# The order of three scales, the first solve's last add and the first T products in a recurrence, expert and feed-forward kernel

## The chip, the cores and the metric

One core of a Trainium2 chip. The metric is device time of the whole program in microseconds, the median of several runs. Three runs of the kernel before gave 1320.99 us as median, with 1320.44 and 1326.19 at the ends.

## The reference

Three stages follow one another: a recurrence over 768 steps for 32 independent heads (4 batches of 8 heads, head size 40), then a mixture of experts with two experts per token, then a feed-forward layer.

```python
for t in range(S):
    y[:, :, t] = einsum('bhd,bhde->bhe', rt, state)
    Sa = einsum('bhde,bhe->bhd', state, at)
    state = state * wt[:, :, None, :] - einsum('bhd,bhe->bhde', Sa, bt)
    state = state + einsum('bhd,bhe->bhde', vt, kt)
...
logits = x @ w_gate + log1p(exp(x @ w_noise)) * noise
top2 = argpartition(-logits, 2)[:, :2]        # two experts per token, relu(x @ w1[e]) @ w2[e]
...
h = x @ w_in
out = (h * tanh(log1p(exp(h)))) @ w_out
```

All of it is computed in float32 precision.

## The kernel before

**The recurrence.** The 768 steps are cut into 24 chunks of 32 steps, and the heads into two groups of 16, so the recurrence proper (`chain`, line 588) is a loop of 48 steps g, two for each chunk. Inside a chunk the 32 steps are coupled by a triangular system; its inverse T turns the chunk into matmuls. Each chunk i goes through these stages, which lie off the loop and have to be ready ahead of it:

- `scale(i)` (line 210) computes running products of the decays w on VectorE with two scans (lines 217 and 221) and a reciprocal (line 220), and multiplies a by them (abd, line 226) and k and b by their inverses (kb, line 230; on VectorE for chunks under 8). Between the last two it issues `load_w` (line 197: two DMAs on SP) for a later chunk into the tile wa that this scale has just read for the last time; for chunks 5, 6 and 7 that is the load for chunks 7, 8 and 9. ScalarE copies the end products into WE (lines 232 and 233), and `decays(i)` (line 237) copies E into Ec (line 240). Scale and decays together are `decayed(i)`.
- `turned(i)` (line 323) is `prods(i)` (line 257: 32 small matmuls on TensorE, line 270, evicted by ScalarE, line 277, one part being sent to DRAM as lscr, line 278), a mask on GpSimd, `turns(i)` (line 288: four groups of four transposes on TensorE, line 294, evicted by ScalarE, lines 300 and 311, one part being sent to DRAM, line 302), the load of a later kb (line 195), and `scale_a(i)` on GpSimd (line 254), which also loads a later AT (line 247).
- `solve_group(k)` (line 390) solves the triangular systems of four chunks at a time on VectorE. It ends with six pairs of a multiplication (line 428) and an add (a reduction along the free axis, line 431). Behind the last add, T is written to DRAM (tscr, line 465), and `tbd(i)` (line 356, the DMAs of line 360) loads it again as diagonal blocks Tbd, four DMAs for each chunk.
- `apply(i)` (line 363) multiplies Tbd with AM on TensorE, in two halves of eight matmuls each (line 377: "T's products"), and ScalarE evicts them into Z (line 379). Step g of the loop starts from Z: `u_mm` (lines 530 and 533), then `s_mm` (line 543), whose result VectorE multiplies by WE into the next state ST (line 548).

**What sets the order.** On TensorE, ScalarE, VectorE and GpSimd the order of the instructions is the order in which the program emits them (`manual_schedule`). On SP, which issues the DMAs, the framework's scheduler orders them by its own estimate of when each is ready. The emission is ruled by a list of positions. Three generators, prepare (scales and products), solve and apply, each give the position of their next piece; `pump(tau)` (line 677) always runs the piece with the lowest position, up to tau. Everything with a position up to t0 = -0.35 is emitted ahead of the loop over g, the rest in slots between the loop's parts.

Ahead of the loop, a piece's position is -1 + x / 42 (`early`, line 314). In the first solve, x is the running sum of the costs that `at` is given in `solve_group`: seven pieces with 0.38 + 0.0083 t t (3.822 in all), eight with 0.6, then 1.2 for each multiplication and each add. So the last two adds stand at x = 20.622 and 21.822, positions -0.5090 and -0.4804. T's products of chunk 0 stand at x = `z0`. The pieces of prepare are listed in `plan`: (1, i, p) is `decayed(i)` and (0, i, p) is `turned(i)` at position p. 

```python
def early(self, x):
    return -1 + x / 42
...
for first, i, at in OPT["plan"]:
    yield at
    for _ in (self.decayed if first else self.turned)(i):
        yield at
...
yield self.tau(at + sg * OPT["zd"]) if i else self.early(OPT['z0'])
```

Behind the recurrence come the experts (`Experts`, with matmuls at lines 1235 and 1254) and the feed-forward layer (`Ffn`, lines 1548 and 1610); the change does not touch them.

Of the kernel before, what the change touches and what calls it, by code (L numbers as in the profile page):

```python
# [24 lines left out]
PR = 8  # L25
NC = S // C
NG = NP * NC
OPT = dict(yd=(), yv=33, gix=(1, 3, 4), ye=(2, 2),  lag2=1, plan=((0, 4, -0.881), (1, 5, -0.499), (1, 6, -0.498), (0, 5, -0.495), (1, 7, -0.493), (0, 6, -0.316), (0, 7, -0.249), (1, 8, -0.020)), dl=0, dk=0, ns=(0, 0), nw=(1, 1), va=1, rb=0, ra=1, kb=0, ry=(2, 2), p1=(0, 0, 0, 1, 1, 1), lw=((4, 2, 2), (6, 6, 6)), fl=((0, 1, 2, 2, 2, 2, 2, 2), (0,) * 8), lag=6, ll=.06, hurry=40, pool=(1, 4), rvpool=False, f=(3, 3, 1, 1, 1, 0), s=(.05, .72), s_1=(-.12, .62), tl=1.9, zl=.96, zd=.32, t0=-.35, nd=3, z0=22)
NW = 2 * PR * (C + 1)
NTB = 2  # L30
GJ = 4
# [34 lines left out]
class Rec:  # L66
# [190 lines left out]
    def prods(self, i):  # L257
# [18 lines left out]
        for out, k in ((ls, 1), (am[:, :, 64:96], 0))[:1 if i < GJ else 2]:  # L276
            nc.scalar.mul(out=out, in_=pv[:, :, k], mul=-1.0)
        (nc.scalar if i < OPT['dl'] else nc.sync).dma_start(out=self.lscr[i // GJ][i % GJ * PR:i % GJ * PR + PR].rearrange("u q t i -> (q t) u i"), in_=ls)

# [8 lines left out]
    def turns(self, i):  # L288
# [12 lines left out]
        self.KN[i] = self.pkn.tile([128, HH * D], F32, name="knd")  # L301
        (nc.scalar if i < OPT['dk'] else nc.sync).dma_start(out=self.KN[i], in_=kn.rearrange("p h d -> p (h d)"))
        if i % 2 == 0:
# [28 lines left out]
    def prepare(self):  # L332
        n = len(self.seq)
        for first, i, at in OPT["plan"]:
            yield at
# [27 lines left out]
    def apply(self):  # L363

        nc = self.nc
        for i in range(len(self.seq)):
            at = 2 * i - OPT["zl"]
            if i and i % GJ == 0:
                yield self.tau(2 * i - OPT["tl"])
                self.tbd(i)  # L370
            self.wants[2] = lambda: 2 if self.solved <= i // GJ else self.ready <= i
            z = self.Z[(i + 2) % 3]
            for sg in range(2):
                yield self.tau(at + sg * OPT["zd"]) if i else self.early(OPT['z0'])
                pt = self.pp.tile([128, 512], F32, name="pp")
# [1332 lines left out]
```

## Time and profile before

| | |
|---|---|
| median of three runs | 1320.99 us (1320.44 to 1326.19) |
| the profiled execution | 1327.01 us, of which the span is 1325.2 us |
| TensorE busy | 1154.2 us (87%) |
| VectorE busy | 872.9 us (66%) |
| ScalarE busy | 704.7 us (53%) |
| GpSimd busy | 573.7 us (43%) |
| granted clock of TensorE, mean | 0.937 of full speed |

The profile is of one execution; its times are microseconds from the start of the span, and the shares of busy time are means over stages with different limits. The recurrence comes first in the span, and its preparation at the very start. Engines in the rows: PE is TensorE, DVE VectorE, ACT ScalarE, POOL GpSimd, SPq the DMA issues of SyncE. "out<-in" are the program's names without buffer numbers; "pp" and "cs" are PSUM tiles. A granted clock of 1.00 is 2.4 GHz, 0.50 is 1.2 GHz.

### The profile page before, as it was taken

How to read it: one execution, taken by the hardware profiler on the slowest of the kernel's cores; microseconds unless marked ns; L12 is line 12 of the kernel's file. 1: busy time of each engine (PE TensorE's matmuls, PEld its weight loads, DVE VectorE, ACT ScalarE, POOL GpSimd, SP SyncE). 2: the span in 40 equal slices, each digit the busy share in tenths (PEclk: the TensorE clock that was granted, in tenths of full speed). 3: DMA queues.
4: the chain of work that ended last, by engine and by line, in shares of the span. 5: the costliest groups of instructions: out<-in, count | busy, mean ns of one | idle time of the engine just before them, and what ended most of it. 6: DMA issues, size and time to landing. Idle time of an engine off the chain costs nothing. (4 is left out here: it accounts for less than half of the span.)

```text
span 1325.2 us, 34053 instructions
## 1 busy us (share of the span) xinstructions
PE 1154.2 (87%) x13902; PEld 1108.1 (84%) x13902; DVE 872.9 (66%) x1601; ACT 704.7 (53%) x1475; POOL 573.7 (43%) x525
## 2 busy tenths in 40 slices
PE   5156788889779797898999999898989999999998
PEld 5146677878678686898999999898989999999998
DVE  8938869595957352646787787585466555665543
ACT  5435566667447365343344344342366766666664
POOL 5223736363336334432244444342355545554331
PEclk9578798999879798899999999898999999999999
DMA  8565585858445657662563564653271111110000
GB/s 237 140 158 130 135 199 136 213 125 205 106 113 107 79 121 125 126 200 76 161 194 113 171 190 131 203 162 123 80 207 31 41 40 31 31 32 19 11 11 21
DMA packets 144989, 156.83 MB, mean 118 GB/s; under 512 B 70954, under 2 KB 113962, under 8 KB 144810
## 3 DMA queue, kind: packets, MB, share of 16 engines
q1 hardware_dynamic: 127594, 120.52, 36.1%
q0 software_dynamic: 10752, 22.32, 6.4%
q10 hardware_dynamic: 6464, 11.54, 3.1%
q8 instruction: 120, 1.97, 0.7%
q14 instruction: 59, 0.48, 0.1%
HBM read 111.20 MB, written 43.12 MB: 116 GB/s over the span
## 5 line engine op out<-in xcount | busy, mean ns | idle before, releaser
L1580 POOL TENSOR_TENSOR gl<-fh,gh 128x1024 fp32r<-128x1024 f32 x46 | 131.0, 2876 | 105.4 <-ACT gh L1596 102.0
L1235 PE MATMUL ph<-xh,w1h 128*128 128x256 f32 (+1 forms) x576 | 160.4, 291 | 8.9 <-issue 8.9
L1235 PE MATMUL ph<-xl,w1h 128*128 128x256 f32 (+1 forms) x576 | 160.1, 291 | 0.0
L1548 PE MATMUL fps<-fxh,ih 128*128 128x256 f32 x576 | 156.4, 286 | 2.0 <-DVE fh L1550 2.0
L1548 PE MATMUL fps<-fxl,ih 128*128 128x256 f32 x576 | 153.8, 281 | 0.5 <-DVE fxl L1091 0.3
L1579 DVE TENSOR_TENSOR fh<-fh,fp 128x1024 f32<-128x1024 f32 x48 | 95.0, 2014 | 60.5 <-ACT fp L1578 60.5
L1254 PE MATMUL py<-w2h,hh 128*128 128x320 f32 x400 | 130.5, 326 | 4.1 <-ACT hh L1087 3.3
L1089 DVE SCALAR_TENSOR_TENSOR hl<-ph,hh 128x512 fp32r<-128x512 f32 (+1 forms) x104 | 69.2, 666 | 89.0 <-ACT hh L1087 88.7
L1254 PE MATMUL py<-w2h,hl 128*128 128x320 f32 x400 | 126.5, 316 | 1.1 <-DVE hl L1089 1.1
L1254 PE MATMUL py<-w2l,hh 128*128 128x320 f32 x400 | 126.3, 316 | 1.3 <-DVE w2l L1091 1.3
L1235 PEld LDWEIGHTS ph<-xh,w1h 128*128 128x128 f32 x576 | 111.8, 194 | 10.0 <-issue 9.8
L1550 DVE COPY fh<-fps 128x512 f32<-128x512 f32 x96 | 64.8, 690 | 79.4 <-ACT fp L1549 74.0
L1610 PE MATMUL fpy<-oh,gl 128*128 128x320 f32 x384 | 114.6, 310 | 0.0
L1610 PE MATMUL fpy<-oh,gh 128*128 128x320 f32 x384 | 114.3, 309 | 0.0
L1610 PE MATMUL fpy<-ol,gh 128*128 128x320 f32 x384 | 113.9, 308 | 0.0
L1235 PEld LDWEIGHTS ph<-xl,w1h 128*128 128x128 f32 x576 | 111.9, 194 | 0.4 <-DVE xl L1091 0.4
L1235 PE MATMUL ph<-xh,w1l 128*128 128x256 f32 (+1 forms) x384 | 111.5, 290 | 0.4 <-DVE w1l L1091 0.4
L1548 PEld LDWEIGHTS fps<-fxh,ih 128*128 128x128 f32 x576 | 109.0, 189 | 2.3 <-DVE fh L1550 2.2
L1548 PEld LDWEIGHTS fps<-fxl,ih 128*128 128x128 f32 x576 | 109.0, 189 | 1.1 <-DVE fxl L1091 1.1
L1548 PE MATMUL fps<-fxh,il 128*128 128x256 f32 x384 | 107.8, 281 | 0.0
L1087 ACT ACTIVATE hh<-ph 128x512 fp32r<-128x512 f32 (+1 forms) x104 | 59.7, 579 | 87.3 <-PE ph L1235 86.2
L1549 ACT ACTIVATE fp<-fps 128x512 f32<-128x512 f32 x96 | 56.0, 596 | 79.3 <-PE fps L1548 75.0
(278 smaller groups left out, 3267.7 us busy)
## 6 DMA issues: line engine op xcount, KB each, us to landing
share<-in_w_dram SPq DMA_DIRECT2D x9, 1280.0 KB
share<-in_w_dram SPq DMA_DIRECT2D x9, 1024.0 KB
wa<-in_wa_dram SPq DMA_DIRECT2D x40, 195.2 KB
knd<-kn SPq DMA_DIRECT2D x24, 320.0 KB
kb<-in_kb_dram SPq DMA_DIRECT2D x40, 192.0 KB
KB<-knd SPq DMA_DIRECT2D x24, 320.0 KB
yb<-y SPq DMA_DIRECT2D x22, 320.0 KB
ST<-in_vn_dram SPq DMA_DIRECT2D x48, 128.0 KB
```

The source lines that it names most:

```text
L1087: nc.scalar.activation(out=hi, in_=src, func=AF.Relu if relu else AF.Copy)
L1089: nc.vector.scalar_tensor_tensor(out=lo, in0=src, scalar=0.0, in1=hi.bitcast(F32), op0=ALU.max, op1=ALU.subtract)
L1235: nc.tensor.matmul(ph[:, m % c], lhsT=a, rhs=b, start=(q == 0), stop=(q == len(ops) - 1))
L1254: nc.tensor.matmul(py, lhsT=a[:, m, ts], rhs=b[:, m], start=(m == 0 and q == 0), stop=(m == FC - 1 and q == 2))
L1548: nc.tensor.matmul(ph[:, i], lhsT=a, rhs=b, start=(q == 0), stop=(q == len(ops) - 1))
L1549: nc.scalar.activation(out=p[:, 2 * m2:2 * m2 + 2], in_=ph, func=AF.Sigmoid, scale=-1.0)
L1550: nc.vector.tensor_copy(h[:, 2 * m2:2 * m2 + 2], ph)
L1579: mul = lambda s: nc.vector.tensor_tensor(out=h[:, s], in0=h[:, s], in1=p[:, s], op=ALU.mult)
L1580: low = lambda s: (nc.vector if last and s.start % 8 else nc.gpsimd).tensor_tensor(out=gl[:, s], in0=h[:, s], in1=gh[:, s].bitcast(F32), o ...
L1610: nc.tensor.matmul(py, lhsT=a[:, m, ts], rhs=w[:, m], start=(q == 0), stop=(q == len(ops) - 1))
```

## The change

Only the table of positions (line 28) is changed; shown are the two entries that differ.

```diff
-plan=((0, 4, -0.881), (1, 5, -0.499), (1, 6, -0.498), (0, 5, -0.495), (1, 7, -0.493), (0, 6, -0.316), (0, 7, -0.249), (1, 8, -0.020))
+plan=((0, 4, -0.881), (1, 5, -0.4512), (1, 6, -0.45), (0, 5, -0.4488), (1, 7, -0.4452), (0, 6, -0.3162), (0, 7, -0.2487), (1, 8, -0.02))
...
-z0=22
+z0=23.2
```

`z0` = 22 is the position -0.4762, and 23.2 is -0.4476. The order of emission between the last two adds of the first solve and the start of the loop is, by these positions:

- before: add (-0.5090), scale 5, scale 6, products and flips of chunk 5, scale 7, last add (-0.4804) with tscr and Tbd of chunk 0, T's products of chunk 0, Tbd of chunk 1;
- after: add (-0.5090), last add (-0.4804) with tscr and Tbd of chunk 0, scale 5, scale 6, products and flips of chunk 5, T's products of chunk 0, Tbd of chunk 1, scale 7.

The pieces at -0.3162, -0.2487 and -0.02 stay in the slots of the loop in which they were.

## Rows read from the trace of the kernel before

**Rows 1.** The page: the span, and VectorE's busy tenths in 40 equal slices (33.1 us each).

```profile
span 1325.2 us, 34053 instructions
...
DVE  8938869595957352646787787585466555665543
```

**Rows 2.** Windows: start:end, length, each engine's busy us and instructions, TensorE's granted clock, DMA share, GB/s.

```profile
59.00:75.00 16.00, 5.17 (x80) 4.15 (x80) 15.79 (x17) 5.42 (x15) 3.62 (x3) 0.50 0.51 129
75.00:81.70 6.70, 0.00 (x0) 0.00 (x0) 0.01 (x1) 0.00 (x0) 0.00 (x0) 0.50 0.63 163
81.70:86.10 4.40, 3.97 (x18) 3.56 (x18) 0.00 (x0) 1.16 (x2) 0.00 (x0) 0.50 0.33 90
86.10:105.00 18.90, 16.88 (x443) 14.53 (x445) 3.45 (x10) 12.77 (x34) 4.88 (x6) 1.00 0.63 159
```

**Rows 3.** Waits, 55 to 100 us: us in total, times, longest.

```profile
PE pp L377 <- DMA Tbd<-tscr: 12.9, 1, 12.9
```

**Rows 4.** Timeline of VectorE: start us, us, line, operation, out<-in [idle before <-releaser].

```profile
59.05 1.24 DVE L217 TENSOR_TENSOR_SCAN E<-wa,d 104x528 f32<-104x528 f32 x1
...
62.38 1.22 DVE L230 TENSOR_TENSOR kb<-kb,R 104x1024 f32<-104x1024 f32 x1
...
68.53 1.25 DVE L217 TENSOR_TENSOR_SCAN E<-wa,d 104x528 f32<-104x528 f32 x1
...
72.67 1.21 DVE L230 TENSOR_TENSOR kb<-kb,R 104x1024 f32<-104x1024 f32 x1
73.80 1.21 DVE L431 TENSOR_REDUCE Tt<-tm 128x128 f32<-128x1024 f32 x1
88.69 0.99 DVE L548 TENSOR_TENSOR ST<-cs,WE 40x320 f32<-40x320 f32 x2 [13.69 <-PE cs L543]
```

**Rows 5.** Timeline of SP's DMA issues, 55 to 130 us.

```profile
62.49 5.67 SPq L195 DMA_DIRECT2D wa<-in_wa_dram  x4
...
72.81 1.00 SPq L195 DMA_DIRECT2D wa<-in_wa_dram  x2
75.04 0.34 SPq L465 DMA_DIRECT2D tscr<-Tt  x1
...
78.41 3.79 SPq L360 DMA_DIRECT2D Tbd<-tscr  x8
```

**Rows 6.** Timeline of TensorE: chunk 5's products and flips, two chunks' T products.

```profile
63.70 1.93 PE L270 MATMUL pp<-kb,abd 40*32 40x64 f32 x64 [18.71 <-issue]
...
67.25 1.63 PE L294 MATMUL pp<-ident,Ec 104*64 104x104 f32 x8
...
81.77 3.70 PE L377 MATMUL pp<-Tbd,share 128*96 128x128 f32 x16 [12.90 <-DMA Tbd<-tscr]
...
99.05 1.11 PE L377 MATMUL pp<-Tbd,share 128*96 128x128 f32 x8
...
100.44 1.04 PE L377 MATMUL pp<-Tbd,share 128*96 128x128 f32 x8
```

**Rows 7.** Timeline of ScalarE, 60 to 89 us: scale 7's copies, T's second eviction, U.

```profile
69.81 0.22 ACT L232 COPY WE<-E 40x16 f32<-40x16 f32 x1 [0.48 <-DVE E L217]
70.04 0.22 ACT L233 COPY WE<-E 40x16 f32<-40x16 f32 x1
70.28 0.62 ACT L240 COPY Ec<-E 104x512 f32<-104x512 f32 x1
...
85.51 0.58 ACT L379 COPY Zt<-pp 96x512 f32<-96x512 f32 x1 [1.13 <-PE pp L377]
86.94 0.86 ACT L533 COPY ST<-cs 32x320 f32<-32x320 f32 x2 [0.85 <-PE cs L530]
```

**Rows 8.** Windows of 1 us: DMA share, the last but one number.

```profile
65.00:66.00 1.00, 1.00 (x27) 0.83 (x20) 0.96 (x2) 0.98 (x4) 0.00 (x0) 0.50 0.15 46
```

**Rows 9.** Windows of the recurrence's first stage, columns as in the second group.

```profile
105.00:210.00 105.00, 79.78 (x1716) 71.63 (x1712) 88.66 (x124) 60.18 (x167) 51.42 (x30) 0.87 0.63 153
...
140.00:160.00 20.00, 12.42 (x246) 11.27 (x241) 17.35 (x18) 7.38 (x21) 14.75 (x7) 0.74 0.44 119
```

More of the change, by code (lines that the diff above doesn't have):

```diff
@@ L27 @@
 NG = NP * NC
-OPT = dict(yd=(), yv=33, gix=(1, 3, 4), ye=(2, 2),  lag2=1, plan=((0, 4, -0.881), (1, 5, -0.499), (1, 6, -0.498), (0, 5, -0.495), (1, 7, -0.493), (0, 6, -0.316), (0, 7, -0.249), (1, 8, -0.020)), dl=0, dk=0, ns=(0, 0), nw=(1, 1), va=1, rb=0, ra=1, kb=0, ry=(2, 2), p1=(0, 0, 0, 1, 1, 1), lw=((4, 2, 2), (6, 6, 6)), fl=((0, 1, 2, 2, 2, 2, 2, 2), (0,) * 8), lag=6, ll=.06, hurry=40, pool=(1, 4), rvpool=False, f=(3, 3, 1, 1, 1, 0), s=(.05, .72), s_1=(-.12, .62), tl=1.9, zl=.96, zd=.32, t0=-.35, nd=3, z0=22)
+OPT = dict(yd=(), yv=33, gix=(1, 3, 4), ye=(2, 2),  lag2=1, plan=((0, 4, -0.881), (1, 5, -0.4512), (1, 6, -0.45), (0, 5, -0.4488), (1, 7, -0.4452), (0, 6, -0.3162), (0, 7, -0.2487), (1, 8, -0.02)), dl=0, dk=0, ns=(0, 0), nw=(1, 1), va=1, rb=0, ra=1, kb=0, ry=(2, 2), p1=(0, 0, 0, 1, 1, 1), lw=((4, 2, 2), (6, 6, 6)), fl=((0, 1, 2, 2, 2, 2, 2, 2), (0,) * 8), lag=6, ll=.06, hurry=40, pool=(1, 4), rvpool=False, f=(3, 3, 1, 1, 1, 0), s=(.05, .72), s_1=(-.12, .62), tl=1.9, zl=.96, zd=.32, t0=-.35, nd=3, z0=23.2)
 NW = 2 * PR * (C + 1)
```

## The prediction

> **What bounds the kernel now.** The page comes first: 1325.2 us of span, and VectorE's slices nearly full from 0 to 80 us, with a hole in the slice after them [rows 1]. The chain that ended last runs through the experts and the feed-forward stage and says nothing of the start, so the start is read from windows. From 59 to 75 us VectorE is busy 15.79 of 16.00 us; from 75.0 to 81.7 us VectorE, TensorE, ScalarE and GpSimd together are busy 0.01 us; then TensorE alone works until 86.1 us [rows 2]. The waits name that hole: TensorE waits 12.9 us at line 377 for the DMA that loads Tbd from tscr [rows 3]. It cannot start without it: the last add of the first solve completes T, T goes to DRAM and comes back as blocks, and no step of the recurrence can run before chunk 0's T products.
>
> The timeline of VectorE shows where that add stands. From 59.05 to 73.88 the engine does the scales of chunks 5, 6 and 7 (five instructions each, the first at 59.05, the last at 72.67 for 1.21 us); the last add runs at 73.80 for 1.21 us; the next VectorE instruction comes 13.69 us later, at 88.69 [rows 4]. So 14.75 us of scales (73.80 - 59.05) lie in front of the one add for which all wait, and 13.7 idle us behind it.
>
> **What the change does, term by term.** Worked out from the numbers of the list, the order on VectorE becomes last add, scales 5, 6, 7. On TensorE it stays: chunk 5's products and flips, then T's products; it is these that have been held together by moving both numbers. On ScalarE the copies of scale 7 move from in front of T's evictions to behind them. On SP the tscr write and the Tbd loads, behind the issues for chunks 7, 8 and 9 until now, come ahead of them in program order.
>
> - **The last add** starts at 59.05 in place of 73.80: 14.75 us earlier, ready at 60.26. By the way through DRAM alone, T's products could start 81.77 - 75.01 = 6.76 us after it [rows 4, 6], at 67.0. The pieces are a tscr issue at 75.04, a first Tbd issue at 78.41 (3.37 later), and T's products 3.36 after that [rows 5, 6].
> - **The scales** come 1.2 us later (one add). That is cheap in itself, but chunk 5's products wait for scale 5 and stand ahead of T's on TensorE. Scale 5's last multiplication ends at 63.60 and the products start at 63.70; the flips end at 67.25 + 1.63 = 68.88 [rows 4, 6]. All of that 1.2 later: TensorE reaches T's products at 70.1. This is later than 67.0, so it decides: **81.77 - 70.1 = 11.7 us earlier**, 3.1 us of the 14.75 given back to chunk 5's products. What hid these products (VectorE's own work on scales 6 and 7) is gone, and this is their price.
> - **ScalarE.** Scale 7's three copies (two for WE, one for Ec) take from 69.81 to 70.90, 1.09 us [rows 7]; now they stand between T's second eviction (end 86.09) and the copy of U into ST (86.94), where 0.85 us are free: **0.24 us lost**. Their input, scale 7's first scan, would be done at 68.53 + 1.25 + 1.2 = 71.0, long before 86.09 - 11.7 = 74.4, so they don't wait.
> - **VectorE behind it.** Scale 7 ends at 72.67 + 1.21 + 1.2 = 75.1, and the first state update is wanted at 88.69 - 11.4 = 77.3: 2.2 us to spare, cost nothing. If that cover is gone, each us of delay of scale 7 beyond 2.2 is paid in full.
> - **SP and the transfers.** Chunk 7's wa loads wait for scale 5's abd product and were issued from 62.49 [rows 5]. They had 6.04 us until scale 7's scan at 68.53, though the transfer share was down to 0.15 between 65 and 66 us [rows 8], so they land about 3 us after the first issue. Now they can go at 63.7 at the earliest, just when the first Tbd load can (78.41 - 14.75 = 63.7). If four Tbd loads go first (eight take 3.79, so 1.9 us [rows 5]), wa goes at 65.6 and lands at 68.6, or by the 6.04 at 71.6, against a scan wanted at 69.7: between 0 and 1.9 us late, within the 2.2 to spare. If wa goes first, Tbd is late by its two issues, 1 us, against 3.1 to spare. Either is taken as 0; the sequence of SP is not written by hand, and is a rival below. Chunk 5's own issues (lscr, knd, the next kb and AT) go 1.2 us later with its products; they are read by the second solve and by chunks 5 to 8, all behind chunk 0.
> - **Clock.** T's sixteen products ran at a granted clock of 0.50 (1.2 GHz) [rows 2] and took 3.70 us; another chunk's took 1.11 + 1.04 = 2.15 at a later time [rows 6]. Bounds: 0 and 1.55 us gained, as they now follow 5.2 us of other matmuls without a gap. I take 0: those same 5.2 us (63.70 to 68.88) stayed at 0.50 to their end [rows 2].
> - **Later order.** The scheduler places the DMA issues of the whole recurrence by its own clock, which has moved; no row prices that. The spread of the three runs shown, 5.7 us, is the nearest measure of what such jitter can do, halved on both sides: -3 to +3; I take 0.
>
> Sum: 14.75 - 3.1 - 0.24 = 11.4 us. All four manual engines, from the first state update on, keep their order, and nothing behind it waits for an absolute time: what follows waits on results of the recurrence. The profiled execution took 1327.0 us (span 1325.2 and 1.8 around it), so 1315.6 of the same kind. It lies 6.0 us above the median of the three runs, 1320.99; against that, 1320.99 - 11.4 = **1309.6 us**.
>
> **The rivals.** What a measurement of this kernel can tell from no change is about 0.5%, 6.6 us.
>
> *T's products at full clock.* They follow directly on chunk 5's work; if the clock rises as they start, 1.55 us more are gained, and 13.0 in all: 1308.0. For it: before, it rose 4.4 us after T's products began, [rows 2] with 81.7 to 86.1 at 0.50 and 1.00 behind. Against it: chunk 5's 5.2 us alone did not raise it. 0.17. The Trainium skill says in "TensorE: Matmul & The Clock Gate", Part 1, that the gate follows how busy TensorE has lately been, counted in time and not in matmuls; by that rule the joined work should rise earlier, and the sum would be 13.0 in place of 11.4. The trace speaks half against it: 5.2 us of nearly unbroken small matmuls left the clock low.
>
> *Tbd behind a load that waits for a scale.* SP stands still at the head of its queue. If the scheduler puts the Tbd loads behind chunk 8's wa loads (which wait for scale 6, last issue until 68.16 [rows 5]), they go at 69.4 and T starts at 72.7: gain 9.1 - 0.2, 1312.1. Behind chunk 9's (until 73.81): Tbd at 75.0, T at 78.4, gain 3.4 - 0.2, 1317.8, which is within 0.5%. For it: before, all six loads are issued ahead of tscr. Against it: that was program order then, and is not now. 0.07 and 0.04. The Trainium skill, in "DMA: Bandwidth & Descriptors", section "Queues, rings and completion order", has each DMA engine take descriptors in the order of its ring; by that, wa's bytes issued ahead of Tbd's delay them even if SP does not wait. That would use about 2 of the 3.1 us to spare and leave 11.4 as it is; no row before shows those two side by side.
>
> *Slower: the clock in the recurrence.* From 105 to 210 us TensorE is busy 79.78 us at a mean clock of 0.87, with a stretch of 20 us at 0.74 inside [rows 9]. If the new phase of its pauses held the whole stage at 0.74, its work would take 79.78 x 0.87 / 0.74 = 93.8, 14.0 more than now, and the kernel would be 2.6 us slower, 1323.6; it decides from a mean of about 0.76 on (79.78 x 0.87 / 0.76 = 91.3, the 11.4 gone). For it: the clock does fall there. Against it: the same matmuls in the same order, moved as a whole. 0.04; slower by over 0.5% needs two such stages, 0.03 with all else.
>
> *The shift is swallowed*, because a later stage, by its transfers or an order of SP that I don't see, ends when it did: 1321. Nothing in the profile shows such a fixed time. 0.06. That the new numbers don't change VectorE's order is excluded by the arithmetic of the positions.
>
> **How the numbers follow.** Forecast 0.62, full clock 0.17, chunk 8 0.07, chunk 9 0.04, swallowed 0.06, slower 0.04. The range goes from the full-clock case less 2.5 us of jitter, 1305.5, to the chunk 8 case with 3, rounded up to 1316. Faster by over 0.5% (under 1314.4): 0.62 + 0.17 + 0.07 less a little for jitter, 0.85; within 0.5%: 0.12; slower: 0.03.
>
> **What would show it.** Right: last add at about 59 us; scales 5 to 7 behind it without a gap until about 75; T's products at 70.1 with TensorE busy up to then, their wait not for Tbd; the first state update at 77.3; everything from there to the end 11.4 earlier. T's products starting at 67 to 70 with a wait on Tbd, or over 70.3 with one, would show the DMA path in charge; a VectorE gap ahead of scale 7's scan would show wa late. Wrong as a whole: the first state update at 77 and yet an end less than 6 us earlier.

## The result, and the profile after

The changed kernel took **1307.62 us** (median of four runs, 1305.80 to 1312.09), the kernel before 1323.32 us with a fourth run added. The ratio is 0.9886, with a 95% interval from 0.9848 to 0.9924. Two later series of the same pair, on chips 3 and 13, gave 0.9915 (0.9883 to 0.9947) and 0.9908 (0.9875 to 0.9940). The kernel before took 1347.57 and 1326.28 us there, so whole times are compared only as ratios or within one chip. The start of the traces repeats across chips (T's products of chunk 0 start at 81.77 and 81.75 in two traces of the kernel before, at 69.29 to 70.20 in three of the changed one), so times of the start are compared across them, to within about 1 us. 11.4 us were forecast. 1307.62 lies 13.4 us under the median of 1320.99 from which the forecast started and 15.7 under the 1323.32 of its own series; the three ratios make 15.1 of 1323.32, 11.5 of 1347.57 and 12.2 us of 1326.28.

The span of the changed kernel's page (shown with VectorE's 40 slices) is 14.9 us shorter, and its third slice, where the hole lay, reads 4 in place of 3 [rows 1]:

```profile
span 1310.3 us, 34057 instructions
...
DVE  8949778695949345448679787584465556655543
```

The windows of its start, with the columns of [rows 2]:

```profile
57.00:69.90 12.90, 5.00 (x81) 4.20 (x81) 12.76 (x14) 3.94 (x11) 0.94 (x1) 0.50 0.38 98
69.90:72.60 2.70, 2.70 (x19) 2.56 (x18) 2.63 (x3) 1.00 (x2) 1.89 (x2) 0.72 0.97 227
72.60:86.00 13.40, 10.89 (x302) 8.81 (x303) 4.22 (x7) 9.75 (x27) 5.68 (x7) 1.00 0.84 195
86.00:94.00 8.00, 6.43 (x158) 5.92 (x152) 1.05 (x3) 4.57 (x12) 0.00 (x0) 1.00 1.09 240
```

No window is left in which all engines stand still: the 6.70 us with 0.01 busy on VectorE and nothing elsewhere [rows 2] are gone. VectorE works 12.76 of 12.90 us up to T's products and 2.63 of 2.70 beside them. The clock is 0.72 on the mean in the window of T's products, where it was 0.50.

VectorE's timeline, with the columns of [rows 4]:

```profile
58.00 2.34 DVE L431 TENSOR_REDUCE Tt<-tm 128x64 f32<-128x1024 f32 x2
60.25 1.25 DVE L217 TENSOR_TENSOR_SCAN E<-wa,d 104x528 f32<-104x528 f32 x1
...
69.72 1.25 DVE L217 TENSOR_TENSOR_SCAN E<-wa,d 104x528 f32<-104x528 f32 x1
...
73.87 1.21 DVE L230 TENSOR_TENSOR kb<-kb,R 104x1024 f32<-104x1024 f32 x1
75.99 0.99 DVE L548 TENSOR_TENSOR ST<-cs,WE 40x320 f32<-40x320 f32 x2 [0.92 <-PE cs L543]
...
86.47 0.99 DVE L548 TENSOR_TENSOR ST<-cs,WE 40x320 f32<-40x320 f32 x2 [0.39 <-PE cs L543]
94.58 0.17 DVE L416 TENSOR_TENSOR tm<-Tt,Lu 128x4 f32<-128x4 f32 x1 [7.12 <-DMA Lu<-lscr]
```

The last add is the second of the two at 58.00 (it ends about 60.3, ahead of scale 5's scan at 60.25); before, it was the row at 73.80 [rows 4]. Scale 7's scan comes at 69.72 and its last multiplication at 73.87, with no idle time in front of either. The first state update is at 75.99, **12.70 us earlier than before** (88.69 [rows 4]), and no longer behind a wait of 13.69. The row at 94.58 is for later.

TensorE's timeline, to be held against [rows 6]:

```profile
64.90 1.93 PE L270 MATMUL pp<-kb,abd 40*32 40x64 f32 x64 [20.72 <-issue]
...
68.44 1.63 PE L294 MATMUL pp<-ident,Ec 104*64 104x104 f32 x8
69.89 2.70 PE L377 MATMUL pp<-Tbd,share 128*96 128x128 f32 x16
```

Chunk 5's products start 1.20 us later than before (63.70), its flips too, and T's products follow at 69.89 without idle time in front of them: they wait for TensorE, not for Tbd, and take 2.70 us in place of 3.70.

The issues on SP, to be held against [rows 5]:

```profile
60.36 0.35 SPq L465 DMA_DIRECT2D tscr<-Tt  x1
...
63.69 0.79 SPq L195 DMA_DIRECT2D wa<-in_wa_dram  x2
64.59 1.84 SPq L360 DMA_DIRECT2D Tbd<-tscr  x4
...
68.16 1.30 SPq L195 DMA_DIRECT2D wa<-in_wa_dram  x2
```

The scheduler has put one pair of wa loads (chunk 7's, at 63.69) between the tscr issue and the four Tbd loads, and chunk 8's behind. ScalarE from T's second eviction on, to be held against [rows 7]:

```profile
72.63 0.58 ACT L379 COPY Zt<-pp 96x512 f32<-96x512 f32 x1 [0.29 <-PE pp L377]
73.11 0.22 ACT L232 COPY WE<-E 40x16 f32<-40x16 f32 x1
73.34 0.23 ACT L233 COPY WE<-E 40x16 f32<-40x16 f32 x1
73.60 0.62 ACT L240 COPY Ec<-E 104x512 f32<-104x512 f32 x1
74.24 0.86 ACT L533 COPY ST<-cs 32x320 f32<-32x320 f32 x2
```

Scale 7's copies stand between the eviction (end 73.21) and the copy of U, which starts 1.03 us later; before, the gap was 0.85.

### The profile page after: what moved, and what is told of

The parts are those of the page before. It is cut to its first block, busy times and chain, and to the rows that moved or that the text cites. A ratio compares the mean times of both kernels' runs of the same rounds, so it can differ in the third digit from the quotient of the medians.

```text
span 1310.3 us, 34057 instructions
## 1 busy us (share of the span) xinstructions
PE 1150.5 (88%) x13902; PEld 1105.6 (84%) x13902; DVE 875.0 (67%) x1601; ACT 705.0 (54%) x1475; POOL 574.0 (44%) x525
## 5 line engine op out<-in xcount | busy, mean ns | idle before, releaser
L254 POOL TENSOR_TENSOR share<-AT,EN 64x320 f32<-64x320 f32 x48 | 58.9, 1228 | 103.2 <-issue 46.5
```

Source lines behind the costliest of these rows:

```text
L254: self.nc.gpsimd.tensor_tensor(out=self.AM[i % (2 * GJ)][64 * ab:64 * ab + 64, :, 0:D], in0=self.AT[r, ab], in1=en[r, ab], op=ALU.mult)
```

## The experiments

All edits are to the table of positions (line 28), but for one line in `solve_group`; e7 is made on the kernel before, the others on the changed one. Runs e1 to e4 are from chip 3, the second trace of the kernel before, e5, e6 and e7 from chip 15, e8 and e9 from chip 13. Times are starts in us from each run's own trace (state updates: line 548); "Lu" is the wait of the second solve for its input, told of further below. The ratio is to the kernel before on the same chip; the two rows of the kernel before are the two traces of it.

| kernel | T's products | first update | second | third | Lu | ratio (95%) |
|---|---|---|---|---|---|---|
| before | 81.77 | 88.69 | 99.16 | 112.17 | 4.09 |  |
| before, again | 81.75 | 89.67 | 104.11 | 116.71 | 3.69 |  |
| changed | 69.89 | 75.99 | 86.47 | 102.50 | 7.12 | 0.9886 (0.9848-0.9924) |
| changed, e1_again | 69.29 | 76.38 | 86.85 | 101.64 | 5.88 | 0.9915 (0.9883-0.9947) |
| changed, e8_changed | 70.20 | 77.07 | 87.55 | 102.68 | 6.22 | 0.9908 (0.9875-0.9940) |
| e2_scale7_only | 80.72 | 87.81 | 98.28 | 111.94 | 4.75 | 0.9988 (0.9963-1.0012) |
| e6_scale7_products_behind | 76.01 | 82.88 | 93.35 | 108.25 | 5.99 | 0.9977 (0.9950-1.0004) |
| e3_scale5_ahead | 71.61 | 79.03 | 89.50 | 104.11 | 5.71 | 0.9931 (0.9903-0.9959) |
| e4_products_in_loop | 68.74 | 75.51 | 89.81 | 105.96 | 7.24 | 0.9931 (0.9906-0.9957) |
| e7_before_solve2_later | 81.96 | 89.39 | 99.86 | 106.28 | none | 0.9979 (0.9954-1.0004) |
| e5_solve2_later | 69.62 | 75.92 | 86.39 | 92.81 | 1.35 | 0.9879 (0.9842-0.9917) |
| e9_solve2_later | 70.17 | 76.71 | 87.18 | 93.60 | 0.66 | 0.9837 (0.9796-0.9879) |

### The pair once more: e1_again and before_again

No edit. The changed kernel:

> The changed kernel itself, once more. Theory A (the gain is made between the last add of the first solve and the first state update, and is worth about 11 to 13 us there; what comes later moves by a few us from execution to execution): last add at 59, T's products at 69.9, first state update at 76.0, ratio to before 0.988 to 0.992. Rival B (part of the 14.9 us between the two profiled spans was luck of one execution in the last third of the recurrence): the first update again at 76.0, but the step updates near 440 to 460 us lose or gain several us against the first profile of this kernel, and the ratio is nearer 0.992.

The kernel before:

> The kernel before, once more, for a second trace on the same chip as the runs below. Theory A: first state update 12 to 13 us later than in the changed kernel on any chip; last add at 73 to 75, T's products 6.8 us behind its end; from the second update on the difference shrinks by 2 to 3 us, because the wait for Lu ahead of the second solve is shorter here (4.1 us against 5.9 and 7.1 in two traces of the changed kernel). Rival B: differences from 440 us on are luck of one execution, and here they are not the 14.3 us of the first two traces.

The start repeats: T's products at 69.29 and the first update at 76.38, against 81.75 and 89.67. The rest does not repeat to the microsecond. In the first pair of traces the difference was 12.7 us at the first update, 9.7 at the third, and 15.4 at the first matmul of the experts (522.63 and 507.19); in the second pair (chips 15 and 3) 13.3, 15.1 and 11.4 (537.68 and 526.29). The spans differ by 14.9 us in the first pair and by 16.7 in the second (1346.9 and 1330.2), where 5.3 of the 16.7 come behind the start of the experts, which the change does not touch. So what one pair of traces shows behind the first update carries several us of luck (rival B); the gain in time is known from the ratios alone, as 11.5 to 15.1 us. One piece of such luck has a row. In the second trace of the kernel before, the window that answers to the last of [rows 2]:

```profile
86.10:105.00 18.90, 18.02 (x319) 15.41 (x320) 2.70 (x6) 8.82 (x23) 4.90 (x6) 0.60 0.48 124
```

The granted clock averaged 0.60 there, where the first trace had 1.00, and from the first to the second update it took 14.44 us (89.67 to 104.11) against 10.47.

Most of the difference between the chips has a place too. Late in the recurrence one update comes 26.7 to 26.8 us behind the one before it in all eight traces from chips 3 and 15 (474.93 to 501.67 in e1_again), and 6.7 to 6.8 in the other four (465.39 to 472.15 in e8_changed). It falls on the changed kernel and the one before alike; its cause was not followed.

### Only scale 7 behind the add: e2_scale7_only

```diff
-(1, 5, -0.4512), (1, 6, -0.45), (0, 5, -0.4488), (1, 7, -0.4452)   z0=23.2
+(1, 5, -0.499), (1, 6, -0.498), (0, 5, -0.495), (1, 7, -0.4452)   z0=22
```

> Only scale 7 goes behind the last add; scales 5 and 6 and chunk 5's products stay ahead of it. By VectorE alone the last add starts 5.3 us earlier than before (68.5 for 73.8) and T's products at 76.5. Theory A with SP's queue: the Tbd loads now stand behind chunk 9's wa loads, which wait for scale 7's abd product (about 73.9), so Tbd is issued at 75.0 and T's products start at 78.3, 3.4 us earlier than before, with a wait on Tbd; first state update at about 85.4; about 3 us faster in all, within 0.5%. Rival C (SP's order doesn't matter, only VectorE's): T's products at 76.5, first update at 83.6, about 5 us faster.

The timeline, all engines, rows on the way of T:

```profile
69.00 1.20 DVE L431 TENSOR_REDUCE Tt<-tm 128x128 f32<-128x1024 f32 x1
...
69.92 2.62 POOL L254 TENSOR_TENSOR share<-AT,EN 64x320 f32<-64x320 f32 x2 [1.93 <-issue]
...
72.57 0.49 SPq L247 DMA_DIRECT2D AT<-in_at_dram  x1
73.16 0.54 SPq L465 DMA_DIRECT2D tscr<-Tt  x1
...
77.06 3.78 SPq L360 DMA_DIRECT2D Tbd<-tscr  x8
...
80.72 3.70 PE L377 MATMUL pp<-Tbd,share 128*96 128x128 f32 x16 [11.39 <-DMA Tbd<-tscr]
...
87.81 0.99 DVE L548 TENSOR_TENSOR ST<-cs,WE 40x320 f32<-40x320 f32 x2 [12.43 <-PE cs L543]
```

The last add starts at 69.00, 4.7 us earlier than in the second trace of the kernel before (73.66), but T's products at 80.72 (78.3 expected), only 1.0 earlier, and the kernel is 0.9988 of before, no change that can be told. Rival C falls. SP held it up, as expected, though one step sooner than I had put it: the tscr issue itself, ready when the add ended at 70.20, went at 73.16, behind the AT load at 72.57, which waits for GpSimd's product to end (69.92 + 2.62 = 72.54).

### The same order on VectorE, another on SP: e6_scale7_products_behind

```diff
-(0, 5, -0.495)   (of the run above)
+(0, 5, -0.478)
```

The position -0.478 lies behind the last add and ahead of T's products; on VectorE nothing changes place.

> As the run with scale 7 alone behind the last add, but chunk 5's products (and with them the issues of lscr, knd, kb and AT on SP) are emitted behind the last add too; VectorE's order is the same as in that run. Theory A with SP's queue: the tscr issue no longer stands behind the AT load that waits for GpSimd, so it goes at 69.8, Tbd at 73.2, T's products start at 76.5 with a wait on Tbd, first update at 83.5, 4 us earlier than with the other order; 4 to 5 us faster than before in all. Rival C (only VectorE's order counts): T's products at the same time as in that run, 80.7.

```profile
68.45 1.21 DVE L431 TENSOR_REDUCE Tt<-tm 128x128 f32<-128x1024 f32 x1
...
69.68 0.35 SPq L465 DMA_DIRECT2D tscr<-Tt  x1
...
72.55 1.93 SPq L360 DMA_DIRECT2D Tbd<-tscr  x4
...
75.54 0.49 SPq L247 DMA_DIRECT2D AT<-in_at_dram  x1
...
76.01 3.48 PE L377 MATMUL pp<-Tbd,share 128*96 128x128 f32 x16 [7.22 <-DMA Tbd<-tscr]
...
82.88 0.99 DVE L548 TENSOR_TENSOR ST<-cs,WE 40x320 f32<-40x320 f32 x2 [8.05 <-PE cs L543]
```

The tscr issue goes at 69.68, right behind the add, and T's products start at 76.01, 4.7 us earlier than in the run above with the same order on VectorE; 0.55 us of that are this trace's earlier add, some 4.2 are SP's. GpSimd's product starts at 69.37, earlier by the same 0.55, so it is not what moved. **This shows that it takes SP's order as well as VectorE's**: of the 4.7 to 5.2 us that the add moved, the first order passed on 1.0 and this one 5.7. In the time it can't be told: 4 to 5 us were expected, and 0.9977 (0.9950 to 1.0004) and 0.9988 (0.9963 to 1.0012) overlap with each other and with 1.

### Scale 5 ahead of the add: e3_scale5_ahead

```diff
-(1, 5, -0.4512), (1, 6, -0.45), (0, 5, -0.4488), (1, 7, -0.4452)   z0=23.2
+(1, 5, -0.499), (0, 5, -0.478), (1, 6, -0.477), (1, 7, -0.4452)   z0=22
```

> Scale 5 stays ahead of the last add, scales 6 and 7 go behind it. Chunk 5's products are then hidden under the solve again, and the way of T through DRAM should decide: last add at 63.6, Tbd issued at about 68.6 (behind chunk 5's knd, which waits for its copies), T's products at 71.9 with a wait on Tbd and mostly at the low clock, first state update at 78.8. Theory A: 2 to 3 us later than the changed kernel at the first update, about 10 us faster than before. Rival D (chunk 5's products in front of T's are a loss in the changed kernel and hiding them pays): T's products at 70 or earlier, first update before 76.

```profile
63.26 1.21 DVE L431 TENSOR_REDUCE Tt<-tm 128x128 f32<-128x1024 f32 x1
...
64.50 0.34 SPq L465 DMA_DIRECT2D tscr<-Tt  x1
...
67.59 0.33 SPq L302 DMA_DIRECT2D knd<-kn  x1
...
68.01 1.98 SPq L360 DMA_DIRECT2D Tbd<-tscr  x4
...
71.61 3.70 PE L377 MATMUL pp<-Tbd,share 128*96 128x128 f32 x16 [3.10 <-DMA Tbd<-tscr]
...
79.03 0.99 DVE L548 TENSOR_TENSOR ST<-cs,WE 40x320 f32<-40x320 f32 x2 [4.28 <-PE cs L543]
```

Chunk 5's products are hidden again, and T's products now wait 3.10 us for Tbd; they start at 71.61 (71.9 expected) and the first update comes at 79.03 (78.8). That is 2.65 us later than in the changed kernel on the same chip. Rival D falls by the trace: the changed kernel's order of scale 5 costs less than the hiding would. The ratios, 0.9931 and 0.9915 on this chip, don't tell the two apart.

### Chunk 5's products in the loop: e4_products_in_loop

```diff
-(0, 5, -0.4488), (1, 7, -0.4452)
+(0, 5, -0.33), (1, 7, -0.325)
```

> The changed order, but chunk 5's products and scale 7 go into the first slot of the loop, behind the first state update, so that T's products have TensorE to themselves. Theory A: T's products start at 68.0 on Tbd's landing (Tbd is issued at 64.6 as in the changed kernel) at the low clock for 3.7 us, first state update at 74.9, 1.1 us earlier than in the changed kernel; but the first pass of the loop then holds two chunks' products instead of one and loses 3.9 us (what chunk 6's took there), so the second update comes at about 89.3 instead of 86.5, and the kernel is 2 to 3 us slower than the changed one. Rival E (the products fit into pauses of the loop): the second update at 85.4, and the kernel beats the changed one by 1 us.

```profile
68.74 3.55 PE L377 MATMUL pp<-Tbd,share 128*96 128x128 f32 x16 [24.06 <-DMA Tbd<-tscr]
...
75.40 1.10 PE L270 MATMUL pp<-kb,abd 40*32 40x64 f32 x64
...
78.85 1.10 PE L270 MATMUL pp<-kb,abd 40*32 40x64 f32 x64
...
83.11 1.10 PE L270 MATMUL pp<-kb,abd 40*32 40x64 f32 x64
...
89.81 0.99 DVE L548 TENSOR_TENSOR ST<-cs,WE 40x320 f32<-40x320 f32 x2 [0.39 <-PE cs L543]
```

T's products start on Tbd's landing at 68.74 (68.0 expected): with TensorE free, the way through DRAM sets the start. From the tscr issue to T's products it is 8.42 us here (60.32 to 68.74) and 9.53 in each of the three traces of the changed kernel (60.36 to 69.89 in the first), so chunk 5's work costs the changed kernel 1.1 us. But three chunks' products (line 270 at 75.40, 78.85 and 83.11) now lie between the first and the second update, where the changed kernel has two, and the second update comes at 89.81, 2.96 later than in e1_again. The ratio is 0.9931 against 0.9915 on the same chip, some 2 us of the expected sign, but within the intervals. Rival E falls by the trace.

### The second solve a slot later: e7_before_solve2_later, e5_solve2_later and e9_solve2_later

The row at 94.58 in VectorE's timeline above waited for Lu, the input of the second solve. The load of Lu on SP and the first operation that reads it, in the kernel before:

```profile
99.62 0.37 SPq L387 DMA_DIRECT2D Lu<-lscr  x1
...
104.24 0.17 DVE L416 TENSOR_TENSOR tm<-Tt,Lu 128x4 f32<-128x4 f32 x1 [4.09 <-DMA Lu<-lscr]
```

On SP in the changed kernel, where the operation is the row at 94.58:

```profile
87.28 0.41 SPq L488 DMA_DIRECT2D RR<-in_rt_dram  x1
87.78 0.37 SPq L387 DMA_DIRECT2D Lu<-lscr  x1
88.21 2.85 SPq L360 DMA_DIRECT2D Tbd<-tscr  x4
```

VectorE stands at the head of its queue for 7.1 us where it stood for 4.1, with scale 8, a product of the loop and the third update behind it. That this wait sets the third update can be read from the table: in each of the nine rows down to e4 the third update comes 8.90 to 8.92 us plus the wait for Lu behind the second (102.50 - 86.47 = 16.03 = 8.91 + 7.12). The edit starts the solve behind the third update and leaves its load where it is:

```diff
-    yield s0 - OPT["ll"]
+    yield -.18 if k == 1 else s0 - OPT["ll"]
...
-s_1=(-.12, .62)
+s_1=(-.0124, .62)
```

In the kernel before:

> The kernel before with the same later start of the second solve. Theory A: the hole for Lu here is only 4.1 us, so at most 4 us are to be had, 2 to 4 us faster than before; if it gains as much as the same edit in the changed kernel, the Lu wait was not what the changed kernel gave back.

In the changed kernel:

> The changed kernel, with the second solve's first operation emitted one slot later on VectorE, behind the third state update, while its load of Lu keeps its place. Theory A (of the gain at the first update 3 us are given back at the third one, because VectorE stands at the head of its queue for Lu with scale 8 and the third update behind it): the wait for Lu falls from 7.1 to about 2 us, the third update comes at 97 to 98 in place of 102.5, the updates up to the seventh 4 to 5 us earlier, and the kernel is 3 to 5 us faster than the changed one. Rival F (the second solve's end decides, and it doesn't come earlier): updates up to the seventh earlier, but T's products of chunk 4 wait for Tbd and the eighth is where it was; same time as the changed kernel.

And once more beside the changed kernel, e8_changed, on one chip:

> The changed kernel, beside the next run on one chip. Theory A: 0.988 to 0.992 of before.

> The changed kernel with the later start of the second solve, beside the run above on the same chip. Theory A: 0.984 to 0.988 of before, 4 to 6 us below the changed kernel (the fourth update to the last by 5 us and more in the first pair of traces: 106.9 against 114.3, 457 against 463). Rival F: the later solve shows at the ends of the other groups, and the two are within 2 us of one another.

e5_solve2_later, SP and VectorE around the load of Lu:

```profile
87.79 0.34 SPq L387 DMA_DIRECT2D Lu<-lscr  x1
...
92.81 0.99 DVE L548 TENSOR_TENSOR ST<-cs,WE 40x320 f32<-40x320 f32 x2
...
95.16 0.17 DVE L416 TENSOR_TENSOR tm<-Tt,Lu 128x4 f32<-128x4 f32 x1 [1.35 <-DMA Lu<-lscr]
```

e9_solve2_later, VectorE there:

```profile
95.25 0.17 DVE L416 TENSOR_TENSOR tm<-Tt,Lu 128x4 f32<-128x4 f32 x1 [0.66 <-DMA Lu<-lscr]
```

The wait is 1.35 and 0.66 us, and the third update comes at 92.81 and 93.60, 9 us earlier than in the changed kernel (101.64, 102.68), more than the 5 expected, since it no longer follows the solve's first operations either: it is 6.42 us behind the second update in both, so 2.5 us are these operations (8.91 - 6.42) and the rest the wait. Beside each other on chip 13, the two kernels took 1312.97 and 1303.93 us, 0.9908 (0.9875 to 0.9940) and 0.9837 (0.9796 to 0.9879) of before. The 9.0 us between them are more than the 4 to 6 expected, and the slowest of the six runs (1308.89) lies below the fastest of the eight (1309.64). Earlier, e1_again on chip 3 and e5 on chip 15 gave 0.9915 and 0.9879, some 5 us apart, with intervals that overlap. Rival F falls: the ninth update is at 156.47 against 166.58, and the gain lasts. In the kernel before, the same edit gives 0.9979 (0.9954 to 1.0004), 2.8 us of 1346.80, which can hardly be told from nothing, though its third update moved by 5.9 us or more (106.28 against 112.17 and 116.71). So the trace of the kernel before gains more than the "at most 4 us" expected there, and its time no more than was expected; where the rest goes was not followed. **The version that beats both kernels is this one**, the changed order with the second solve a slot later.

## Why the prediction was right

- **The last add** was to start at 59.05 and be ready at 60.26; the tscr issue that follows it went at 60.36. Right.
- **Chunk 5's products decide.** T's products at 70.1 were forecast, 69.89 came, with TensorE busy up to them and no wait for Tbd; in e3, where the products are out of the way, T waits for Tbd and starts later (its add too is later, at 63.26), and in e4 the way through DRAM gives 68.74 where 67.0 was the bound without SP's wa loads. So the 3.1 us "given back to chunk 5's products" was the right choice of the two bounds, though the true distance between them is 1.1 us, not 3: the Tbd loads went 0.9 later than the earliest 63.7, behind chunk 7's wa loads, which the forecast had named as one of the two orders, and in e4 T's products came 4.19 us behind the first Tbd issue (64.55) in place of 3.36.
- **ScalarE** lost 0.18 us (1.03 against 0.85), forecast 0.24. The 0.85 depends on the clock, though: in the second trace of the kernel before, where the clock was still at 0.50 there, ScalarE stood idle 1.36 us between the two, and against that nothing is lost.
- **VectorE behind it** was free: scale 7 ended at 75.08 (75.1 forecast), the first update came at 75.99. Only 0.9 us were to spare, not 2.2, as the update came earlier than thought.
- **Clock.** Taken as 0, with 1.55 as the other bound. T's products took 2.70, 3.70 and 3.48 us in the three executions of the changed kernel that were traced, so 1.0, 0 and 0.2 us were gained: the lower bound occurs, the upper one does not, and neither of the two cases, the forecast and the rival at full clock, is the whole truth. In the first trace the first update came 1.3 us ahead of the forecast (75.99 for 77.3); 1.0 of that is the clock, and 0.2 T's earlier start.
- **Tbd behind a waiting load.** This rival did not come about in the change, but it is real: in e2 the tscr issue, a step ahead of Tbd, stood behind a load that waited for another engine, and T's products came 4.7 us later than in e6, some 4.2 of them by SP.
- **What lies behind.** "Nothing behind it waits for an absolute time" held, but the shift was not carried whole: the difference of 12.7 us at the first update was 9.7 at the third, and the wait for Lu, 7.1 us against 4.1, is those 3.0. The forecast had put what SP's new order does under jitter, 0 with 3 on both sides; this part of it is a wait with a place. The load of Lu was issued 1.31 us behind the second update (86.47 to 87.78) in place of 0.46 (99.16 to 99.62), with the load of RR ahead of it, and four Tbd loads went behind it. The 8 us around it, 98 to 106 in the kernel before:

```profile
98.00:106.00 8.00, 6.95 (x168) 6.33 (x167) 3.23 (x12) 5.24 (x13) 0.39 (x1) 1.00 0.62 160
```

  The transfer share there is 0.62, against 1.09 from 86 to 94 us in the changed kernel (the last of its windows above; the profile's count can pass 1), and Lu took 6.80 us from issue to use (87.78 to 94.58) in place of 4.62 (99.62 to 104.24). Over the nine rows of the table down to e4, Lu took 4.62 and 4.63 us where no Tbd load was issued right behind it, 5.30 with one (e2) and 5.78 to 6.80 with four. That the denser traffic is the cause is read from these rows and was not tried by itself; that the wait held back the third update is shown by the constant 8.91 us and by e5 and e9.
- **One reading** was loose: TensorE does not work alone from 81.7 to 86.1 us; ScalarE is busy 1.16 us there [rows 2], with T's evictions. Nothing in the sum hangs on it.

The mechanism held: the add moved ahead of the scales, chunk 5's products set T's start, and the hole closed. The 11.4 us came out close (11.5 to 15.1 by the ratios of the three series) as a sum in which the clock gave up to 1.0 more and Lu took up to 3 back, with a wander of several us behind; that the total lies so near is in part luck. Where that wander comes from, step by step, stays open.

## What to carry to other kernels

Behind a result that all engines wait for, look at what its own engine does just ahead of it: work that is needed later belongs behind it, into the round trip that the result has to make, and the price is what else waits for that work. Moving it on the compute engine is only half: the issue of the transfer has its own queue, and one load in front of it that waits for a third engine can take most of the gain at that place (T's products 1.0 us earlier in e2, 5.7 in e6; the two whole times could not be told apart). And once such a hole is closed, look for the next place where an engine stands at the head of its queue for a load with ready work behind it; here that second step was worth another 9 us on chip 13, and some 5, not clear of noise, by the earlier runs.

## What the hardware showed that I had not expected

The clock of TensorE rose at different places in executions of one program: in the changed kernel within T's products (2.70 us), or behind them (3.70 us); in the kernel before right behind T's products in one trace and only inside the first pass of the loop in the other, with a mean of 0.60 against 1.00 from 86.1 to 105 us. That pass took 4 us more there, from the first update to the second. From 89 to 101 us of that trace TensorE was busy 12.00 of 12.00 us, on small matmuls and transposes, at a granted clock of 0.50 throughout.
